# Another order of the steps of a fused RWKV attention and gated MLP kernel, with PSUM tiles of their own for idle bursts and for the last unit's halves

## The chip, the cores and the metric

The kernel runs on one core of a Trainium2 chip. The time is the device time of one execution in microseconds (us), and of several executions the median. Five engines work side by side, each in the order of its own queue: TensorE (PE: matmuls, with the weight loads shown apart as PEld), VectorE (DVE), ScalarE (ACT), GpSimd (POOL) and SyncE (SP, which here only issues DMAs). They wait for each other by semaphores.

## The reference

Two things are computed one after the other: a linear attention with a decaying state for 4 batches, 8 heads, 768 steps and a head width of 48, and a two-layer network on its result (3072 tokens, 384 wide, 2048 hidden).

```python
for t in range(S):
    cur = np.einsum('bhd,bhe->bhde', u[None] * kt, vt)
    y[:, :, t] = np.einsum('bhd,bhde->bhe', rt, state + cur)
    state = w[None, :, :, None] * state + np.einsum('bhd,bhe->bhde', kt, vt)
x = np.ascontiguousarray(attn_out.transpose(0, 2, 1, 3)).reshape(B * S, H * D)
h = x @ w_in
g = np.where(pos, h, np.where(neg, 0.0, (h + beta) ** 2 / (4.0 * beta)))
return (g @ w_out).astype(np.float32)
```

Here `pos` is h >= 1 and `neg` is h <= -1.

## The kernel before

**Tiles.** The 768 steps are cut into 6 chunks of 128. A *unit* is one chunk of one batch (24 of them, n = 0 to 23), a *group* is two units, one chunk of two batches (12 of them, g = 0 to 11; unit n belongs to group n // 2). Group g = 0 and 1 are the first chunk of all four batches. In a chunk the recurrence is matmuls: r and k are scaled by powers of w (Rs, Ks), transposed, multiplied into a 128x128 matrix A per head, masked (AT) and multiplied with v; the state is carried from chunk to chunk.

**Steps.** The whole program is a list of words, `ORDER` (lines 24 to 60). A loop at line 573 goes through it and calls for each word a function `do_...`, which issues the instructions of that step. So the place of a word in `ORDER` sets its place in the queue of its engine, and nothing reorders it later. `Ks1.0=G` is step Ks for group 1, unit half 0, on GpSimd; V, A and G stand for VectorE, ScalarE and GpSimd; the numbers behind a slash are the PSUM tiles that the step takes. A step waits for the data it reads and for the last reader of the tile that it takes. Some 680 words make the 4051 instructions.

The steps of a group, with the lines that the profile names:

- LR, LK, LV (line 253, SP's queue): loads of r, k, v, in two halves for the first groups, whole later.
- KU, RKU (282), us (304), V (308, the cast of v to bf16, line 112), B (313): the term with u. Rs, Ks (282): the scaled r and k.
- TR, TK, T (330, PE) with cR, cK, c (112): transposes of Rs and Ks for groups 0 to 2; later groups use DMA transposes RT, KT (318).
- A or AA (370, PE), AT (379, or 384 in halves; VectorE), Y (432, 438, PE), y or yg (446, 450; VectorE): the attention's result of a unit or group.
- Sp (405, PE), Tm or Tmg (409, 413; VectorE), decayg (416), sbf or sbfg: the state.
- X and xc (460, 112) or xcg (467, a DMA transpose): y transposed, as tile xT.
- m (475, PE): a quarter q of the hidden layer, 12 matmuls into tile hp; r (486 on ScalarE, 483 on VectorE as a clamp), s (495 or 493, ScalarE), g (498, VectorE): the activation; g reads hp last and frees it.
- M (512, PE): g times w_out for unit j and quarter q, into tile op; og, o (112): op to SBUF; stg, st (558, 555): the store.

`m4.0` is quarter 0 of group 4, `M4.01` is unit 0, quarter 1 of group 4.

**The head.** bw and bu (207, 211) spread log w and u over the partitions by matmuls, wq (233) makes the powers for the state; Wup, Wdn (215, 219) write exp tables to PSUM, WupS, WdnS (222, 225) to SBUF for later groups. WI and WO (244, 247) are the loads of the weights, in three parts each, cast on the way, from GpSimd's queue. `Z` (566) is a burst of matmuls on zeros into tile z.

**PSUM.** Two pairs of banks, p0 and p1, stand for the whole run. The other four banks are single ones, b0 to b3, until the first step takes pair 2 or 3; from then on they are those two pairs. All the steps above that use PSUM share the tiles by these numbers. In the last group the output of a unit has a tile of its own, and the last unit is computed in two halves of 192 columns (MA, MB, and M with both), which both lie in one tile; oA, oB copy them out, stA, stB store them.

Of the kernel before, what the change touches and what calls it, by code (L numbers as in the profile page):

```python
# [40 lines left out]
Sp9 AT11 Tmg4 m4.1/3 s4.0=A Y10/0 Y11 yg5 m4.2/2 r4.1 g4.0 xcg5 RT6 s4.1=A g4.1 m4.3/0 r4.2 us6 KT6 r4.3 LV8 s4.2=A  # L41
g4.2 M4.00/1 M4.10 M4.01 stg0 M4.11 s4.3=A g4.3 m5.1/3 Ks7=G V7 M4.12 LR8 decayg4=G Rs7=G AA6/02 M4.02 M4.03 M4.13
r5.1 AT12 m5.0/0 s5.1=A V6 sbfg4=A stg2 AT13 Y12/2 Y13 stg1 og4=V m5.2/1 g5.1 KU8=G B6=G yg6 m5.3/3 KT7 xcg6 Sp10/2
r5.0 s5.0=A KU7=G RKU7=G r5.2 s5.2=A Sp11 g5.0 M5.00/0 M5.10 M5.11 M5.01 RT7 Tmg5 LR9 g5.2 M5.02 Ks8=G LK9 us7 r5.3
s5.3=A V8 g5.3 decayg5=G sbfg5=A LK11 m6.1/2 r6.1 s6.1=A stg3 Rs8=G RT8 B7=G AA7/13 M5.03 Rs9=G M5.12 M5.13 AT15
m6.0/3 og5=A r6.0 AT14 g6.1 Y14/0 Y15 yg7 RKU8=G KU9=G xcg7 s6.0=A m6.3/1 m6.2/2 g6.0 Sp12/0 Sp13 r6.3 r6.2 s6.2=A us8
KT8 M6.00/3 M6.10 M6.11 M6.01 Tmg6 LV11 B8=G s6.3=A m7.1/0 RT9 LK10 g6.2 M6.02 LV10 g6.3 AA8/21 M6.03 r7.1 M6.12 M6.13
decayg6=G AT16 sbfg6=A RKU9=G LR10 s7.1=A AT17 Ks9=G og6=A m7.0/2 Sp14/1 Sp15 Y16/3 Y17 r7.0 g7.1 m7.2/0 KU11=G s7.0=A
Tmg7 yg8 xcg8 Ks10=G KT9 r7.2 m7.3/1 g7.0 M7.00/3 s7.2=A g7.2 M7.10 M7.11 LV9 r7.3 M7.01 KU10=G s7.3=A g7.3 V10 stg6
decayg7=G M7.12 RKU10=G sbfg7=A M7.02 AA9/02 M7.13 m8.0/1 stg5 LR11 AT18 Rs10=G V9 KT10 M7.03 r8.0 s8.0=A AT19 RT10  # L50
og7=V us9 B9=G m8.1/0 m8.2/2 r8.1 s8.1=A Y18/3 Y19 stg7 g8.0 m8.3/1 yg9 r8.2 Rs11=G RKU11=G M8.00/3 M8.10 xcg9 g8.1
M8.11 s8.2=A g8.2 Sp16/0 Sp17 Tmg8 stg4 RT11 r8.3 s8.3=A M8.01 M8.02 g8.3 m9.0/2 r9.0 s9.0=A us10 decayg8=G AA10/01
AT21 Ks11=G M8.03 sbfg8=A B10=G AT20 M8.12 M8.13 g9.0 og8=A m9.1/1 Y20/0 Y21 r9.1 m9.2/3 s9.1=A yg10 xcg10 g9.1 r9.2
M9.00/0 m9.3/2 KT11 s9.2=A stg8 M9.10 M9.11 Sp18/1 Sp19 r9.3 g9.2 s9.3=A M9.01 Tmg9 M9.02 g9.3 m10.0/3 decayg9=G V11
# [20 lines left out]
def kernel(  # L75
# [485 lines left out]
    def do_Zs(e, b):  # L561
        tiles["z"] = pair(b[0], F32, "z")

    def do_Z(e, b, n):
        for i in range(n):
            nc.tensor.matmul(tiles["z"][:, 0, :P], idle[:, :P], idle[:, :P], start=True, stop=True)  # L566

    def do_Zq(e, b, n):
        for i in range(n):
            nc.tensor.matmul(tiles["z"][:, 0, :D], idle[:, :P], idle[:, :D], start=True, stop=True)  # L570
# [40 lines left out]
```

## Time and profile before

| | us |
|---|---|
| median of 3 runs | 174.13 |
| lowest and highest | 174.08, 174.55 |
| span of the profiled execution | 172.6 |
| busy: PE, DVE, ACT, POOL | 164.4, 130.6, 129.9, 117.4 |

The page gives the span of the profiled execution, from its first to its last instruction, and no other time for it; the runs' median lies 1.5 us above the span. Busy times are sums over the span. A row of a timeline reads: start, length (us), engine, line, operation, out<-in, shapes, count, and in brackets the idle time ahead of it with what ended it. A row of a chain reads: start, length, what. The granted clock of TensorE is 1.00 throughout.

### The profile page before, as it was taken

The page shows a single profiled execution, that of the slowest core. Times are in us where ns is not written, and L with a number is a line of the kernel's source. Part 1 is how long each engine was busy: PE and PEld are TensorE (multiplying, and loading weights), DVE is VectorE, ACT ScalarE, POOL GpSimd, SP SyncE. Part 2 cuts the span into 40 slices and gives each one's busy share as a digit, 9 for nine tenths or more (in the row PEclk, how much of TensorE's full clock was granted, in tenths as well). Part 3 has the DMA queues.
Part 4 walks back from the last instruction along what each step waited for, and adds up shares of the span by engine and source line. Part 5 has one row for each costly group of instructions (what it writes and reads, how often), then busy time and mean ns, then how long its engine had stood idle before and what let it go on. Part 6 is the DMA issues. An engine that isn't in the chain of part 4 may idle for free.

```text
span 172.6 us, 4051 instructions
## 1 busy us (share of the span) xinstructions
PE 164.4 (95%) x1674; PEld 132.9 (77%) x1674; DVE 130.6 (76%) x150; ACT 129.9 (75%) x150; POOL 117.4 (68%) x86
## 2 busy tenths in 40 slices
...
GB/s 114 194 184 179 199 187 180 228 210 174 206 191 99 206 184 168 194 199 145 196 312 210 182 220 163 223 182 155 297 170 267 4 52 145 37 104 0 8 91 91
DMA packets 103751, 28.26 MB, mean 164 GB/s; under 512 B 98866, under 2 KB 102836, under 8 KB 103732
## 3 DMA queue, kind: packets, MB, share of 16 engines
...
q10 hardware_dynamic: 148, 0.10, 0.2%
...
## 4 chain that ended last, share of the span: by engine, by line
PE 87%; ACT 4%; DMA 2%; DVE 2%; issue 1%; POOL 0%; ACTq 0%; DVEq 0%
PE hp L475 35%; PE op L512 34%; PE A L370 4%; PE Y L438 3%; DMA xT<-y 2%; PE Y L432 2%; PE Sp L405 2%; PE z L566 2%; ACT pt L486 1%; PE T L330 1%; ACT TT L112 1%; PE lwp L207 1%; PE wp L233 1%; PE TR L330 1%; PE TK L330 1%
## 5 line engine op out<-in xcount | busy, mean ns | idle before, releaser
L475 PE MATMUL hp<-xT,w_in 128*128 128x256 bf16 x576 | 69.1, 273 | 1.3 <-DMA xT<-y 0.8
L512 PE MATMUL op<-w_out,g 128*128 128x384 bf16 (+1 forms) x400 | 68.4, 320 | 0.0
L498 DVE SCALAR_TENSOR_TENSOR g<-sq,hp 128x1024 bf16<-128x1024 bf16 x48 | 57.9, 1215 | 13.2 <-ACT sq L495 13.2
L475 PEld LDWEIGHTS <-w_in 128*128 128x128 bf16 x576 | 61.9, 114 | 4.6 <-issue 1.6
L486 ACT ACTIVATE pt<-hp 128x1024 f32<-128x1024 f32 x46 | 46.9, 1021 | 13.7 <-PE hp L475 13.7
L512 PEld LDWEIGHTS <-g 128*128 128x128 bf16 x400 | 37.5, 98 | 20.4
L495 ACT ACTIVATE sq<-pt 128x1024 bf16<-128x1024 f32 x46 | 48.3, 1057 | 1.2
L379 DVE TENSOR_TENSOR AT<-A,umask 128x1024 bf16<-128x1024 f32 x20 | 23.7, 1220 | 5.2 <-PE A L370 5.2
L282 POOL TENSOR_TENSOR Ks<-Ki,Wdn 128x768 bf16<-128x768 f32 (+1 forms) x12 | 20.3, 1689 | 8.5 <-ACT Wdn L225 3.4
L313 POOL TENSOR_TENSOR V<-Vb,diag 128x768 f32<-128x768 bf16 (+1 forms) x14 | 18.1, 1291 | 9.8 <-DVE diag L304 4.4
L282 POOL TENSOR_TENSOR RKU<-Ri,KU 128x768 f32<-128x768 f32 (+1 forms) x13 | 21.2, 1630 | 1.1 <-DVE KU L282 0.7
L282 POOL TENSOR_TENSOR KU<-Ki,u_sb 128x768 f32<-128x768 f32 (+1 forms) x13 | 21.2, 1634 | 0.4 <-DMA Ki<-in_k_dram 0.4
L416 POOL TENSOR_TENSOR state<-Tm,wCm 128x768 f32<-128x768 f32 x8 | 14.6, 1824 | 9.8 <-DVE Tm L413 9.8
L282 POOL TENSOR_TENSOR Rs<-Ri,Wup 128x768 bf16<-128x768 f32 x10 | 18.2, 1820 | 0.3 <-DMA Ri<-in_r_dram 0.3
L112 ACT CAST Vb<-Vi 128x768 bf16<-128x768 f32 (+1 forms) x14 | 10.2, 733 | 5.4 <-DMA Vi<-in_v_dram 5.4
L450 DVE TENSOR_TENSOR y<-Y,V 128x768 bf16<-128x768 f32 x10 | 9.6, 956 | 5.9 <-PE Y L438 3.3
L304 DVE TENSOR_REDUCE diag<-RKU 128x16 f32<-128x768 f32 (+1 forms) x14 | 11.6, 831 | 1.5 <-POOL RKU L282 1.5
L112 ACT CAST state_bf<-state 128x768 bf16<-128x768 f32 (+1 forms) x12 | 8.5, 717 | 4.4 <-POOL state L416 4.4
L112 ACT COPY o<-op 128x768 f32<-128x768 f32 (+1 forms) x9 | 6.7, 748 | 6.0 <-PE op L512 5.9
L438 PE MATMUL Y<-Vb,AT 128*128 128x48 bf16 x192 | 10.4, 186 | 0.4 <-ACT Vb L112 0.4
L438 PEld LDWEIGHTS <-AT 128*128 128x128 bf16 x192 | 9.5, 98 | 0.7 <-issue 0.5
L413 DVE TENSOR_TENSOR Tm<-Sp,state 128x768 f32<-128x768 f32 x8 | 7.7, 956 | 3.1 <-PE Sp L405 3.1
...
## 6 DMA issues: line engine op xcount, KB each, us to landing
...
Ki<-in_k_dram SPq DMA_DIRECT2D x6, 192.0 KB, 4.0
Ri<-in_r_dram SPq DMA_DIRECT2D x6, 192.0 KB, 4.7
Vi<-in_v_dram SPq DMA_DIRECT2D x6, 192.0 KB, 6.0
...
```

Of the source, the lines that this page charges most:

```text
L112: nc.scalar.copy(out, in_) if e == "A" else engines[e].tensor_copy(out, in_)
L282: engines[e].tensor_mul(part(out)[:, :, :, :D], part(a), rep(b, j1 - j0) if len(b.shape) == 3 and b.shape[1] == H else part(b))
L304: nc.vector.tensor_reduce(d[:, hs], tiles["RKU", g][:, hs, :], AX.X, ALU.add)
L313: engines[e].tensor_mul(t[:, hs, :], tiles["V", g][:, hs, :], tiles["diag", g][:, hs].unsqueeze(2).to_broadcast([P, n, D]))
L379: nc.vector.tensor_mul(t.rearrange("p i n t -> p (i n) t"), tiles["A", n].rearrange("p i (n t) -> p (i n) t", t=P), umask.unsqueeze(1).to_ ...
L416: engines[e].tensor_mul(states[g % BP], tiles["Tm", g], flat(wCm).unsqueeze(1).to_broadcast([P, UNITS, DM]))
L438: nc.tensor.matmul(Y[:, h * D : (h + 1) * D], AT[:, i, p, :], V[:, j * H + h, :], start=(c == 0), stop=True, skip_group_check=True,)
L475: nc.tensor.matmul(hp[:, f, :], w_in_sb[wi][:, i, wo * FG * P + f : (wo + 1) * FG * P : FG], tiles["xT", g][:, :, i, :], start=(i == 0), s ...
L486: nc.scalar.activation(t, tiles["hp", g, q], AF.Relu, bias=0.5, scale=0.5)
L495: nc.scalar.activation(t, p, AF.Square)
L498: nc.vector.scalar_tensor_tensor(out=make("g", ("g", g, q), [P, FG, TOK], BF16), in0=tiles["sq", g, q], scalar=1.0, in1=tiles["hp", g, q], ...
L512: nc.tensor.matmul(tiles[key][:, i, : o1 - o0], tiles["g", g, q][:, f, j * P : (j + 1) * P], w_out_sb[wi][:, wo, f * DO + o0 : f * DO + o1 ...
```

## The change

All words of `ORDER` are put in another order, and some steps change their engine. The numbers of steps per engine, before and after: VectorE 138 and 154, ScalarE 149 and 141, GpSimd 76 and 67, PE 235 and 233, SP 83 and 84. VectorE gets, of steps that others did, three Ks, one Rs, two RKU, two decayg, three B, the clamps r1.3, r4.2, r9.0, r10.3 and r11.1 (r1.2 goes), most of the early copies cR and cK, and oA; it gives og4 and og10 to ScalarE. GpSimd casts V0.0 and V1.1 (so far all casts of v were on ScalarE).

The list up to the first output matmuls, around group 4's transposed y, and at the end:

```diff
-Zs/0 ln Z19 bw/1 LK0.0 bu/0 uS=V LK1.0 LR0.0 LK0.1 LR0.1 LV0.0 wq/2 WdnS Ks1.0=G LR1.0 LR1.1 Wdn/3 Ks0.0=V Ks0.1=V
-TK0/0 Wup/1 Rs0.0=V TR0/3 LK1.1 cK0=A WupS KU0.1=G KU0.0=V RKU0.0=G cR0=A KU1.0=G LV0.1 Rs0.1=V Z2 TR1/1 A0/03 LV1.0
-LV1.1 WI0 WI1 WI2 us0.0 cR1=A TK1/1 cK1=A AT0.1 Z4 A1/13 Rs1.0=V LR2.0 LR2.1 Rs1.1=V V0.1 AT1.0 V0.0 Z9 TR3/1 B0.0=G
-AT1.1 RKU0.1=V wE AT0.0 wC=A us0.1 Z7 Y1/3 TR2/0 B0.1=G Y0/2 y0 y1 cR2=A RKU1.0=G Z8 X0/2 Z4 TK2/3 X1/0 Ks1.1=G xc0=A
-Sp1/2 cK2=A xc1=A Z7 TK3/3 cK3=A Tm1 A2/20 m0.0/0 cR3=V us1.0 AT2.1 AT2.0 r0.0=A A3/31 AT3.1 KU1.1=G RKU1.1=G m0.1/1
-V1.0 s0.0=A B1.0=G Sp2/2 AT3.0 us1.1 r0.1=A Tm2 Y2/3 y2 g0.0 V1.1 X2/0 LK2.0 Y3/1 B1.1=G s0.1=A LK2.1 Sp0/2 Sp3/3
-xc2=V LK3 y3 WO0 WO1 m0.3/0 r0.3=A s0.3=A g0.1 X3/1 Tm0 xc3=V m0.2/1 LR3 LV2.0 Tm3 m1.1/2 g0.3 r1.1=V m1.0/3 m1.2/0
-Ks2=G r0.2=A s0.2=A g0.2 sbf2=A s1.1=A r1.0=A s1.0=A sbf3=A g1.1 m1.3/1 r1.2=V WO2 KU2=G LV2.1 M0.00/2 M0.10 M0.11
+ln=A LR0.1 LK0.0 Z17/0 bu/1 LR0.0 LK0.1 LV0.1 LV0.0 bw/3 uS=V KU0.0=V LK1.0 LK1.1 Wup=A/1 RKU0.0=V Wdn=A/0 KU0.1=G
+RKU0.1=G us0.0=V V0.0=G wq/2 Ks0.1=V Ks0.0=V Rs0.0=V LR1.0 wE=A WdnS=A Rs0.1=V WupS=A Zp16/0 TR1/1 V0.1=A us0.1=V
+TK1/0 TR0/3 B0.1=V cR1=V B0.0=V Ks1.0=V wC=A cR0=A TK0/1 WI0 Ks1.1=V LR1.1 LV1.0 KU1.1=G cK0=A cK1=V KU1.0=G LV1.1
+Z5/2 A0/21 A1/30 AT0.0=V LK2.0 AT1.0=V AT1.1=V Rs1.0=V WI1 AT0.1=V LK2.1 Zp9/0 Y1/2 Sp0/3 TK3/0 LR2.1 LR2.0 Y0/1 Tm0=V
+cK3=V y1=V LR3 y0=V Zp10/1 X1/2 X0/0 TR2/1 RKU1.0=G V1.0=A xc1=A us1.0=V cR2=V Rs1.1=G WI2 V1.1=G WO1 TK2/2 xc0=A
+Zp3/0 TR3/1 cK2=V RKU1.1=V LK3 Sp2/3 LV2.0 A2/20 LV2.1 LV3 cR3=A m0.0/0 r0.0=A AT2.0=V Tm2=V AT2.1=V s0.0=A A3/13
+AT3.1=V B1.0=V Y2/2 m0.1/1 AT3.0=V y2=V Z9/0 X2/3 g0.0=V Sp1/1 r0.1=A s0.1=A Y3/0 xc2=V us1.1=V m0.3/0 B1.1=G g0.1=V
+y3=V r0.3=A Sp3/3 X3/2 Tm1=V xc3=V m0.2/1 LK4 LK5 LV5 LR4 Tm3=V s0.3=A WO0 m1.1/3 r0.2=A WO2 LR5 m1.0/2 g0.3=V s0.2=A
+r1.1=V s1.1=A sbf1=A r1.0=A g0.2=V s1.0=A Ks2=G KU2=G g1.1=V m1.2/0 m1.3/1 M0.11/3 RKU2=G r1.3=V g1.0=V Rs2=V r1.2=A
+s1.3=A s1.2=A M0.01 M0.00 M0.10 M1.11/2 M1.01 M0.03 M0.12 M0.02 g1.2=V g1.3=V T5/0 M0.13 T4/1 sbf2=A c5=A M1.10 A5/0
+c4=A M1.12 us2=V A4/1 Rs3=G Ks3=V KU3=G AT5=V sbf0=A og0=A M1.13 M1.02 T6/0 AT4=V c6=V V2=A B2=G Y5/3 Sp5/1 Y4 Sp4
 ...
-LV6 r3.0 s3.0=A Ks5=G g2.3 M2.03 Sp6/3 Sp7 M2.13 g3.0 m3.2/0 Rs5=G Tmg3 r3.1 s3.1=A RT5 og2=A g3.1 V4 AA4/23 AT9 Ks6=G
-r3.2 s3.2=A KT5 m3.3/1 M3.00/3 M3.10 V5 B4=G AT8 Y8/2 Y9 r3.3 g3.2 s3.3=A LK8 M3.11 M3.12 M3.01 M3.02 yg4 AA5/20 g3.3
-M3.13 M3.03 xcg4 m4.0/1 LR7 KU5=G RKU5=G AT10 LK7 decayg3=G sbfg3=A Rs6=G og3=A us5 LV7 B5=G KU6=G RKU6=G r4.0 Sp8/2
+m3.3/3 AT9=V M3.01/0 M3.00 LV4 KT5 LK6 RT5 LK8 AT8=V decayg3=G V4=A r3.2=A s3.2=A g3.2=V Y8/2 r3.3=A Y9 V5=A B4=G
+yg4=V M3.10 M3.12 s3.3=A M3.11 M3.02 AA5/21 xcg4 sbfg3=A RKU5=G g3.3=V M3.13 M3.03 us5=V KU6=G AT11=V AT10=V m4.0/3
 ...
-m11.1/0 M10.02 M10.03 r11.1 s11.0=A m11.2/1 g11.0 M10.12 M10.13 s11.1=A r11.2 g11.1 m11.3/2 og10=V s11.2=A M11.10/0
-M11.11 g11.2 stg10 r11.3 s11.3=A M11.00/3 M11.01 M11.12 M11.02 g11.3 M11.03 MA11.13 MB11.13 o11.0=V st11.0 oA11.1=A
-stA11.1=A oB11.1=V stB11.1
+m11.2/0 s10.3=A r11.0=A s11.0=A g10.3=V M10.03 g11.0=V m11.1/2 r11.1=V r11.2=A M10.10 M10.12 m11.3/3 M10.13 M10.02
+s11.2=A g11.2=V M11.02/0 M11.00 s11.1=A g11.1=V r11.3=A s11.3=A M11.01 g11.3=V og10=A M11.10/12 M11.11 MA11.13 M11.03
+M11.12 o11.0=V stg10 st11.0 MB11.13 oA11.1=V oB11.1=V stA11.1 stB11.1
```

In the code, the cast of v takes its engine from the list; the last unit's halves get a PSUM tile each, and the first matmul of an accumulation is found by counting, since the quarters may come in any order; an idle burst takes a tile when it runs (Z a single bank in the head, Zp a pair) where before one tile of pair 0 was taken once by Zs:

```diff
-        copy("A", t[:, hs, :], tiles["V32", g][:, hs, :])
+        copy(e or "A", t[:, hs, :], tiles["V32", g][:, hs, :])
...
-        key = ("op", g, j) if last else ("op", g)
-        if key not in tiles:
-            tiles[key] = pair(b[0], F32, "op")
...
         for i, o0, o1 in [(i, i * DO // 2, (i + 1) * DO // 2) for i in halves] if last and j else [(j, 0, DO)]:
+            key = ("op", g, j, i) if last else ("op", g)
+            if key not in tiles:
+                tiles[key] = pair(b.pop(0), F32, "op")
+            n = counts["op", g, j, i] = counts.get(("op", g, j, i), 0) + 1
...
-                    start=(q == 0 and f == 0), stop=(q == nQ - 1 and f == FG - 1),
+                    start=(n == 1 and f == 0), stop=(n == nQ and f == FG - 1),
...
-    def do_Zs(e, b):
-        tiles["z"] = pair(b[0], F32, "z")
+    def idling(t, n):
+        for i in range(n):
+            nc.tensor.matmul(t, idle[:, :P], idle[:, :P], start=True, stop=True)
...
     def do_Z(e, b, n):
-        for i in range(n):
-            nc.tensor.matmul(tiles["z"][:, 0, :P], idle[:, :P], idle[:, :P], start=True, stop=True)
...
+        idling(pair(b[0], F32, "z")[:, 0, :P] if later else bank(b[0], [P, P], F32, "z"), n)
+
+    def do_Zp(e, b, n):
+        idling(pair(b[0], F32, "z")[:, 0, :P], n)
```

The bursts before are Z19, 2, 4, 9, 7, 8, 4 and 7 (60 matmuls), after Z17, Zp16, Z5, Zp9, Zp10, Zp3 and Z9 (69).

More of the change, by code (lines that the diff above doesn't have):

```diff
@@ L40 @@
-M3.13 M3.03 xcg4 m4.0/1 LR7 KU5=G RKU5=G AT10 LK7 decayg3=G sbfg3=A Rs6=G og3=A us5 LV7 B5=G KU6=G RKU6=G r4.0 Sp8/2
[L41 to L54, printed above, removed]
@@ new lines @@
+decayg5=G r5.2=A M5.11/1 s5.2=A g5.2=V RT7 xcg6 r5.3=A us7=V M5.01 M5.00 M5.10 s5.3=A V7=A m6.1/2 M5.02 Rs8=G KU8=G
+sbfg5=A r6.1=A g5.3=V B7=G Ks8=G s6.1=A AA7/03 AT15=V AT14=V M5.13 M5.03 M5.12 m6.0/3 LK9 LR10 Y14/0 Y15 g6.1=V LK10
+RT8 LV8 LR9 yg7=V og5=A m6.2/1 Sp12/2 r6.0=A m6.3/0 s6.0=A g6.0=V Sp13 r6.2=A KU9=G Rs10=G RKU8=G xcg7 KT8 M6.10/3
+M6.01 M6.11 M6.00 s6.2=A r6.3=A g6.2=V Tmg6=V s6.3=A g6.3=V M6.02 m7.1/1 AA8/02 us8=V V8=A r7.1=A M6.12 M6.13
+decayg6=G B8=G Ks9=G RKU9=G AT16=V AT17=V s7.1=A M6.03 sbfg6=A Rs9=G m7.0/0 og6=A Y17/3 KU10=G Sp15/2 g7.1=V Y16
@@ new lines @@
+sbfg8=A s9.0=A og8=A m9.1/0 Y21/3 Y20 r9.1=A g9.0=V m9.2/1 yg10=V s9.1=A g9.1=V RKU11=G r9.2=A M9.10/2 m9.3/3 us11=V
+Sp19/0 s9.2=A M9.01 M9.11 Sp18 r9.3=A stg8 M9.00 KT11 stg5 xcg10 RT11 g9.2=V Tmg9=V s9.3=A g9.3=V M9.02 m10.0/0 B11=G
+AA11/13 decayg9=V AT23=V r10.0=A sbfg9=A s10.0=A M9.03 M9.13 M9.12 AT22=V m10.1/3 og9=A g10.0=V Y22/1 Y23 m10.2/0
+r10.1=A yg11=V s10.1=A xcg11 stg7 m10.3/2 stg9 g10.1=V r10.2=A M10.00/1 M10.11 M10.01 r10.3=V s10.2=A g10.2=V m11.0/3
+m11.2/0 s10.3=A r11.0=A s11.0=A g10.3=V M10.03 g11.0=V m11.1/2 r11.1=V r11.2=A M10.10 M10.12 m11.3/3 M10.13 M10.02
@@ L528, in half_out @@
     def half_out(e, g, j, i):
-        copy(e, make("o", ("o", g, j, i), [P, UNITS, DO], F32)[:, 0, : DO // 2], tiles["op", g, j][:, i, : DO // 2])
+        copy(e, make("o", ("o", g, j, i), [P, UNITS, DO], F32)[:, 0, : DO // 2], tiles["op", g, j, i][:, i, : DO // 2])
     def do_oA(e, b, g, j):
```

26 lines of the change are left out of this document (14 added, 12 removed).

## The prediction

> **What bounds the kernel now.** The page first: the span, and who is busy in it.
>
> ```profile
> span 172.6 us, 4051 instructions
> PE 164.4 (95%) x1674; PEld 132.9 (77%) x1674; DVE 130.6 (76%) x150; ACT 129.9 (75%) x150; POOL 117.4 (68%) x86
> ```
>
> The 95% of PE is an average over two very different stages, so the chain that ended last comes next, in order of time (start, length, what), and then the table by stage.
>
> ```profile
> 27.27 6.73 PE hp L475 x60
> ...
> 68.81 0.96 DVE y L450
> 69.80 4.27 DMA xT<-y
> 74.11 1.47 PE hp L475 x12
> ...
> 169.14 0.33 ACT o L112
> 169.49 0.36 DVE o L112
> ```
>
> ```profile
> 10.73:27.27 16.54, 14.29 (x180) 12.68 (x179) 13.84 (x25) 10.26 (x19) 10.81 (x14) 1.00 1.12 187
> 27.27:69.10 41.83, 41.83 (x438) 33.57 (x438) 34.04 (x35) 35.12 (x41) 34.84 (x21) 1.00 1.09 185
> 74.10:163.86 89.76, 89.75 (x922) 73.48 (x922) 69.95 (x66) 75.62 (x80) 61.48 (x36) 1.00 0.82 156
> ```
>
> The columns after the length of the stretch are PE, PEld, DVE, ACT, POOL busy. From 27.27, where step m0.2 starts, PE is busy 41.83 of 41.83 and 89.75 of 89.76 us. In that part no order of steps can gain more than PE's idle time there, and the view of PE's waits after 27 us has, beside m0.2's own wait for g0.1, one row:
>
> ```profile
> PE hp L475 <- DMA xT<-y: 0.8, 1, 0.8
> ```
>
> That is m4.0 at 74.11, which waits for group 4's transposed y. So three things can move the end: when the gap-free part is entered, the 0.84 us before 74.11, and the 3.5 us after PE's last matmul. Before 27.27 PE is not the bound: the idle bursts keep it busy with nothing. VectorE is: 13.84 of 16.54 us.
>
> **Part 1, the entry: a sum along VectorE.** In the new order m0.2 stands behind X3, which needs y3, which stands in VectorE's queue behind g0.1. I add up VectorE's queue up to y3. In-order work without waits costs the step from one start to the next, which is less than the duration that a row shows:
>
> ```profile
> 8.27 0.55 DVE L282 TENSOR_TENSOR KU<-Ki,u_sb 128x384 f32<-128x384 f32 x1
> 8.74 0.54 DVE L282 TENSOR_TENSOR Rs<-Ri,up_t 128x384 bf16<-128x384 f32 x1
> ...
> 18.74 0.41 DVE L112 COPY TT<-TR 128x512 bf16<-128x512 bf16 x1
> 19.07 0.54 DVE L304 TENSOR_REDUCE diag<-RKU 128x8 f32<-128x384 f32 x1
> 19.53 1.28 DVE L384 TENSOR_TENSOR AT<-A,umask 128x512 bf16<-128x512 f32 x2
> ...
> 26.00 1.21 DVE L498 SCALAR_TENSOR_TENSOR g<-sq,hp 128x1024 bf16<-128x1024 bf16 x1
> ```
>
> Steps: a half product 0.47 (8.27 to 8.74), a cR or cK 0.33 (18.74 to 19.07), a us 0.46, an AT half 0.60 (two in 1.28, the last lasting 0.68), an xc taken like a cR; a g its full 1.21.
>
> The sum starts at Ks0.1, which needs the fourth load (its issue, and the time to landing of the loads in flight at 2.65) and dn_t (pieces of the chain, and ACT's timeline):
>
> ```profile
> 2.65 0.82 SPq L253 DMA_DIRECT2D Ki<-in_k_dram  x1
> Ki<-in_k_dram SPq DMA_DIRECT2D x1, 192.0 KB, 4.4
> ```
>
> ```profile
> 3.44 1.64 PE lwp L207 x2
> 5.09 1.28 PE up L211 x2
> ...
> 5.60 0.55 ACT L219 ACTIVATE dn_t<-lwp,dn_col 128x384 f32<-128x384 f32 x1
> ```
>
> LK0.1 is fourth in SP's queue in both orders, so it lands at 2.65 + 4.4 = 7.05. The new order puts bu ahead of bw; with u_row there by about 3.0, bw ends near 3.0 + 1.64 + 1.28 = 5.9 instead of 5.08, and the second exponential, dn_t, ends 1.06 after that (as 5.60 + 0.55 = 6.15 comes 1.06 after 5.09), at 6.95. The 0.8 us lost by that swap is hidden by the load. Ks0.1 starts at 7.1.
>
> From Ks0.1 to y3 VectorE gets 17 half products and sums (four Ks, three Rs, one RKU, three B, four y, two Tm): 17 x 0.47 = 8.0; three us 1.4; eight AT halves 4.8; five cR/cK 1.65; two g 2.4; one xc 0.35. Together 18.6, so y3 would end at 25.7 without a wait. Waits that I find by setting the queues beside each other: 0.25 at AT0.0 (A0 now stands behind four sets of transposes and Z5, four matmuls of 0.107 us each, see the idle bursts below), 0.4 at cR2 (TR2 behind Zp10, X1 and X0), 0.2 at cK2 (TK2 waits for the bank that ACT reads in xc1), 0.15 in small ones: 1.0. So y3 ends at 26.7, X3 starts at 26.75, m0.2 at 26.9 (three transposes, 0.17). Against 27.27 that is **0.37 us earlier**. Bounds: no wait at all, 1.0 earlier still; each of these 36 operations at its full duration (0.08 more apiece), 2.9 later. I take the steps, since they are measured in a queue as full as this one.
>
> What else the entry needs. WI2 has to be there for m0.3, which must end by 26.75:
>
> ```profile
> 10.79 2.48 POOL L244 DMA_DIRECT2D w_in<-in_moe_w_in_dram  x3
> w_in<-in_moe_w_in_dram POOLq DMA_DIRECT2D x1, 768.0 KB, 12.6
> q0 software_dynamic: 1200, 1.57, 62.5%
> ```
>
> Before, the three issues stand together and the last lands at 12.4 + 12.6 = 25.0, 14.2 us after the first issue, for the 1.57 MB of q0 in that window: 0.11 MB/us. After, POOL has KU0.1, RKU0.1 and the V0.0 cast ahead of WI0, two KU ahead of WI1, RKU1.0 and Rs1.1 ahead of WI2: issues near 9.9, 13.3 and 16.1. A transfer of 0.39 MB takes 3.5 us at that rate, so each issue comes about when the transfer before it ends, and the last lands between 9.9 + 14.2 = 24.1 and 25 again. Cost 0, but if it came at 26 the entry would come a us later. POOL's cast of a half V is not in the trace: VectorE's half copy (0.41 at 18.74) and POOL's half product (0.99 at 9.85, below) bound it; I take 0.82, POOL's half B, and the time between WI0's landing and m0.0 hides it. V1.1 is twelfth in SP's queue in both orders; POOL's cast of it and B1.1 end by 25.9, before y3 is reached. V0.1 rises from tenth to fifth load, LR1.1 falls from eighth to tenth, and POOL asks for it only at 15.1.
>
> **Part 2, the middle.** VectorE gets four more clamps (as wide as a g, 1.21), six full products that POOL did and two fewer output copies (both taken as a y, 0.96): 4.8 + 5.8 - 1.9 = 8.7 us more in 131.6, on 104.0 busy (34.04 + 69.95): 86%. POOL and ACT get less. So no engine passes PE. The new queues are tightest around 36 us, where g1.0 ends some 0.15 before M1.11 wants its pair. The wait before 74.11: between Y9 and m4.0 stand six M, an AA: 4.45 us, the same list in both orders, against 0.96 + 0.03 + 4.27. It stays. In the other groups at least 4.57 us stand there, against 0.99 and a median of 3.0:
>
> ```profile
> xT<-y SPq DMA_TRANSPOSE x9, 3.0
> ```
>
> I take 0 for the middle; bounds: 0.84 less, 1.5 more.
>
> **Part 3, the end.** oA reads a tile that MB writes after it was ready, so ACT starts it at 169.14, after MB, and oB follows it at 169.49. With a tile for each half, oA needs only the first half's matmuls and ends before MB does; oB starts at 169.14. **0.35 us less.** og10, which M11.10 waits for, stands behind r11.3 and s11.3 on ACT and ends some 2.95 us after m11.3; five M of 0.65 stand before M11.10, 3.25. The margin is 0.3.
>
> The sum: -0.37 + 0 - 0.35 = -0.7 on 172.6, so a span of 171.9. The page gives no time for the profiled execution but its span; the median, 174.13, lies 1.5 above it, and with that 1.5 kept the time is **173.4**. Less than 0.3% (0.5 us) can't be told from no change.
>
> **The rivals.** *VectorE and POOL in each other's way.* Before, VectorE's products with both inputs in SBUF fall where POOL does no arithmetic, but for one pair of rows (below a half product of POOL, and the group of a full one):
>
> ```profile
> 9.85 0.99 POOL L282 TENSOR_TENSOR KU<-Ki,u_sb 128x384 f32<-128x384 f32 x1
> ...
> 13.93 0.55 DVE L282 TENSOR_TENSOR RKU<-Ri,KU 128x384 f32<-128x384 f32 x1
> 14.36 0.82 POOL L313 TENSOR_TENSOR V<-Vb,diag 128x384 f32<-128x384 bf16 x1 [1.10 <-ACT w_col L236]
> ```
>
> ```profile
> L282 POOL TENSOR_TENSOR Rs<-Ri,Wup 128x768 bf16<-128x768 f32 x10 | 18.2, 1820 | 0.3 <-DMA Ri<-in_r_dram 0.3
> ```
>
> The last two of the timeline overlap by 0.12 us, with usual durations, which says little; POOL's full product takes 1.82. The new order puts such products beside POOL's work: B0.1 beside the V0.0 cast, Ks1.1 beside KU1.1 (both released by one load), Rs1.0 beside RKU1.0. If whichever starts second has to wait, VectorE loses 0.3, 0.9 (part of a 0.99 us KU) and 0.85 less what its waits above swallow, some 1.6 us, straight into y3, and Rs2 and Ks3 can lose up to 1.82 each behind full POOL products near 36 to 41 us, where there is no margin. That gives 173.4 + 1.6 = 175.0. It decides from 0.4 us of blocking on. The Trainium skill, SBUF — State Buffer, section "Who interferes with whom", states it as a rule: a VectorE instruction with two SBUF inputs and a GpSimd instruction that reads SBUF exclude each other, and the second waits for the whole of the first. By that rule the time is 175.0; no run here shows it yet. I give it 0.3.
>
> *PE still at half clock when m0.0 comes.* The idle bursts show the change:
>
> ```profile
> 15.87 1.03 PE L566 MATMUL z<-idle 128*128 128x128 bf16 x8
> ...
> 18.00 0.55 PE L566 MATMUL z<-idle 128*128 128x128 bf16 x7
> ```
>
> Less the last one's own 0.28 and 0.22, eight stand 0.107 apart and the later seven 0.055. If that came 2 us later, m0.0 would take 1.3 longer: 174.7. Against it: as dense a PE from 12 us on as before. 0.06.
>
> *Nothing to be seen*: VectorE waits 0.4 more in the head, or the middle gives back what the end gains: 174.0. Half a dozen hand-overs between engines in the head that I set right behind each other speak for it. 0.22.
>
> *More*: the wait before 74.11 goes as well, with loads in another order beside group 4's transfer: 172.6. 0.12.
>
> **Numbers.** The forecast 0.30 (its own range 172.9 to 173.6), more 0.12, nothing 0.22, blocking 0.30, half clock 0.06. Faster 0.42, same 0.22, slower 0.36. The range takes in "more" and blocking with a little of the middle's: 172.4 to 175.6.
>
> **What would show it.** y3 ending at 26.7 and m0.2 starting at 26.9; the half product still 0.47 apart on VectorE beside a busy POOL (a Ks1.1 or Rs1.0 that lasts over 0.6 or starts late without another cause is the blocking); WI2 landing by 25; one PE wait of 0.8 before m4.0; oA over before MB ends. I am wrong if m0.2 starts after 27.3, or if PE shows waits of over 0.3 between 27 us and the last unit other than m4.0's.

## The result and the profile after

The kernel after takes **179.02 us** (median of 4 runs, 178.53 to 180.34) against 174.11 us for the kernel before (4 runs): a ratio of 1.0288, 95% interval 1.0247 to 1.033. It is slower; the prediction said 173.4 and a range up to 175.6. Medians here are of all executions; the ratios leave out single executions in a slower state, of which a0 (182.43) and f2 (184.16) below had one each. The head of the profiled execution (178.53 us) reads:

```profile
span 176.5 us, 4053 instructions
PE 164.7 (93%) x1683; PEld 132.3 (75%) x1683; DVE 145.7 (83%) x166; ACT 125.3 (71%) x143; POOL 105.3 (60%) x77
...
PE 68%; DVE 17%; ACT 5%; DMA 4%; issue 3%; ACTq 0%; DVEq 0%
```

From m0.2 on PE does the same work, in a span 3.9 us longer; the third line is the chain that ended last by engines, in which VectorE had 2% before and now has 17%. The table by stage from m0.2's start to PE's last matmul, first of the kernel before, then of the kernel after (length, then PE, PEld, DVE, ACT, POOL busy):

```profile
27.27:169.10 141.83, 140.99 (x1442) 113.40 (x1441) 111.14 (x106) 113.94 (x123) 101.24 (x59) 1.00 0.88 163
```

```profile
29.00:173.25 144.25, 141.49 (x1443) 112.83 (x1440) 120.48 (x113) 112.03 (x122) 91.74 (x53) 1.00 0.83 155
```

The 3.9 us of the span split by these rows: m0.2 starts at 29.00 in place of 27.27 (**+1.73**); PE is idle 2.76 us behind it in place of 0.84 (**+1.92**) and busy 0.50 longer; from PE's last matmul to the span's end it takes 3.25 in place of 3.5 (-0.25). Why PE is busy 0.50 longer was not followed up. The median moved by a further 1.0: 0.5 is that the profiled execution was the fastest of the four (178.53 against 179.02), and 0.5 that its time lies 2.0 above its span, where the median before lay 1.5 above the span of an execution whose own time is not on record.

**The entry.** The timeline of the kernel after, VectorE's rows first, then POOL's and PE's (in brackets the idle time ahead of a row and what ended it):

```profile
8.46 1.01 DVE L285 TENSOR_TENSOR Rs<-Ri,up_t 128x384 bf16<-128x384 f32 x2
...
11.31 2.62 DVE L285 TENSOR_TENSOR Ks<-Ki,Wdn 128x384 bf16<-128x384 f32 x2
13.85 0.41 DVE L115 COPY TT<-TK 128x512 bf16<-128x512 bf16 x1
...
16.16 0.55 DVE L285 TENSOR_TENSOR Rs<-Ri,Wup 128x384 bf16<-128x384 f32 x1
...
28.06 0.55 DVE L449 TENSOR_TENSOR y<-Y,V 128x384 bf16<-128x384 f32 x1
```

```profile
11.20 2.31 POOL L285 TENSOR_TENSOR KU<-Ki,u_sb 128x384 f32<-128x384 f32 x2 [0.74 <-DMA Ki<-in_k_dram]
...
16.19 0.80 POOL L247 DMA_DIRECT2D w_in<-in_moe_w_in_dram  x1
```

```profile
14.32 0.61 PE L373 MATMUL A<-TT 48*128 48x128 bf16 x8 [1.73 <-DVE TT L115]
```

Two half products on VectorE take 1.01 us when one input lies in PSUM (the look-up table `up_t`), and 2.62 when both lie in SBUF (Ks1.0 and Ks1.1, table `Wdn`) and POOL multiplies beside them. The copy cK1 stands behind the pair, and PE stands 1.73 us for it before A1. Rs1.0, with the same kind of inputs, takes its usual 0.55 at 16.16: POOL is issuing a DMA just then.

**The middle.** PE's waits behind 28 us, where the kernel before had one of 0.8 (the third row ends the entry: X3 for y3):

```profile
PE op L515 <- DVE g L501: 1.2, 1, 1.2
PE hp L478 <- DMA xT<-y: 0.9, 1, 0.9
PE X L463 <- DVE y L449: 0.7, 1, 0.7
PE Y L435 <- DVE o L115: 0.5, 1, 0.5
```

The timeline around the first of them:

```profile
59.50 1.84 POOL L285 TENSOR_TENSOR KU<-Ki,u_sb 128x768 f32<-128x768 f32 x1
59.57 2.58 DVE L285 TENSOR_TENSOR RKU<-Ri,KU 128x768 f32<-128x768 f32 x1
61.30 2.52 POOL L285 TENSOR_TENSOR Rs<-Ri,Wup 128x768 bf16<-128x768 f32 x1
62.08 1.21 DVE L501 SCALAR_TENSOR_TENSOR g<-sq,hp 128x1024 bf16<-128x1024 bf16 x1
...
63.34 0.99 PE L515 MATMUL op<-w_out,g 128*128 128x384 bf16 x5 [1.20 <-DVE g L501]
```

RKU4, a full product with two SBUF inputs, takes 2.58 us on VectorE; the gate behind it is late, and so is PE. When POOL is at rest such a product takes 0.95: Rs2 and Ks3, for which the prediction had feared. POOL has nothing to do from 36.6 to 38.5 and from 40.5 to 46.0, and where its KU3 overlaps the end of Rs2 by 0.34, it is KU3 that takes 2.02 in place of 1.83:

```profile
37.88 0.95 DVE L285 TENSOR_TENSOR Rs<-Ri,Wup 128x768 bf16<-128x768 f32 x1
42.37 0.95 DVE L285 TENSOR_TENSOR Ks<-Ki,Wdn 128x768 bf16<-128x768 f32 x1
```

```profile
34.75 1.83 POOL L285 TENSOR_TENSOR Rs<-Ri,Wup 128x768 bf16<-128x768 f32 x1
38.49 2.02 POOL L285 TENSOR_TENSOR KU<-Ki,u_sb 128x768 f32<-128x768 f32 x1 [1.91 <-DMA Ki<-in_k_dram]
45.96 1.48 POOL L316 TENSOR_TENSOR V<-Vb,diag 128x768 f32<-128x768 bf16 x1 [5.45 <-ACT Vb L115]
```

The wait of 0.9 is for the transposed y of group 7, not of group 4 as before. Two pieces of the chain that ended last:

```profile
106.54 4.95 DMA xT<-y
111.54 1.50 PE hp L478 x12
```

**The clock.** The table by stretches of 1 us (last columns: granted clock, DMA share, GB/s):

```profile
14.00:15.00 1.00, 0.68 (x10) 0.49 (x11) 0.90 (x3) 0.00 (x0) 0.98 (x2) 0.66 1.23 231
15.00:16.00 1.00, 1.00 (x10) 0.84 (x8) 1.00 (x2) 0.00 (x0) 1.00 (x2) 0.50 1.29 228
```

PE stands still from 12.6 to 14.3, and right behind it the granted clock falls to 0.50 until about 17.7. The kernel before is at half clock there too (its idle bursts stand 0.107 us apart up to 17), and VectorE, on which the entry hangs, has between 10 and 28.6 us only two waits of over 0.15 us for PE, of 0.27 and 0.17. So this stretch explains little of the later entry; what did lengthen the entry is the pair.

### The profile page after: what moved, and what is told of

It is laid out like the page before. It is cut to its first block, busy times and chain, and to the rows that moved or that the text cites. A ratio compares the mean times of both kernels' runs of the same rounds, so it can differ in the third digit from the quotient of the medians.

```text
span 176.5 us, 4053 instructions
## 1 busy us (share of the span) xinstructions
PE 164.7 (93%) x1683; PEld 132.3 (75%) x1683; DVE 145.7 (83%) x166; ACT 125.3 (71%) x143; POOL 105.3 (60%) x77
## 3 DMA queue, kind: packets, MB, share of 16 engines
HBM read 20.45 MB, written 4.72 MB: 143 GB/s over the span
## 4 chain that ended last, share of the span: by engine, by line
PE 68%; DVE 17%; ACT 5%; DMA 4%; issue 3%; ACTq 0%; DVEq 0%
PE op L515 29%; PE hp L478 27%; DVE g L501 4%; PE A L373 3%; DMA xT<-y 3%; ACT pt L489 2%; DVE Ks L285 2%; PE Y L441 2%; PE Y L435 2%; DVE AT L387 2%; DVE RKU L285 1%; PE Sp L408 1%; ACT sq L498 1%; DVE AT L382 1%; DMA u_row<-in_u_dram 1%
## 5 line engine op out<-in xcount | busy, mean ns | idle before, releaser
L489 ACT ACTIVATE pt<-hp 128x1024 f32<-128x1024 f32 x42 | 42.9, 1021 | 14.3 <-PE hp L478 14.1
L498 ACT ACTIVATE sq<-pt 128x1024 bf16<-128x1024 f32 x42 | 44.4, 1057 | 1.2
L316 POOL TENSOR_TENSOR V<-Vb,diag 128x768 f32<-128x768 bf16 (+1 forms) x11 | 15.6, 1418 | 21.7 <-DVE diag L307 12.4
L285 POOL TENSOR_TENSOR KU<-Ki,u_sb 128x768 f32<-128x768 f32 (+1 forms) x13 | 21.8, 1680 | 7.3 <-DVE RKU L285 4.7
L285 POOL TENSOR_TENSOR RKU<-Ri,KU 128x768 f32<-128x768 f32 (+1 forms) x11 | 19.2, 1743 | 1.0 <-DMA Ri<-in_r_dram 0.8
L419 POOL TENSOR_TENSOR state<-Tm,wCm 128x768 f32<-128x768 f32 x6 | 11.0, 1827 | 11.7 <-DVE Tm L416 11.6
L285 POOL TENSOR_TENSOR Ks<-Ki,Wdn 128x768 bf16<-128x768 f32 x9 | 16.4, 1829 | 0.0
L285 POOL TENSOR_TENSOR Rs<-Ri,Wup 128x768 bf16<-128x768 f32 (+1 forms) x9 | 16.3, 1812 | 0.0
L115 ACT COPY o<-op 128x768 f32<-128x768 f32 x10 | 8.0, 802 | 6.1 <-PE op L515 6.1
L115 ACT CAST Vb<-Vi 128x768 bf16<-128x768 f32 (+1 forms) x12 | 9.1, 774 | 4.0 <-DMA Vi<-in_v_dram 4.0
```

Of the source, the lines that this page charges most:

```text
L115: nc.scalar.copy(out, in_) if e == "A" else engines[e].tensor_copy(out, in_)
L285: engines[e].tensor_mul(part(out)[:, :, :, :D], part(a), rep(b, j1 - j0) if len(b.shape) == 3 and b.shape[1] == H else part(b))
L316: engines[e].tensor_mul(t[:, hs, :], tiles["V", g][:, hs, :], tiles["diag", g][:, hs].unsqueeze(2).to_broadcast([P, n, D]))
L419: engines[e].tensor_mul(states[g % BP], tiles["Tm", g], flat(wCm).unsqueeze(1).to_broadcast([P, UNITS, DM]))
L489: nc.scalar.activation(t, tiles["hp", g, q], AF.Relu, bias=0.5, scale=0.5)
L498: nc.scalar.activation(t, p, AF.Square)
```

## The experiments

My theory from here on was: VectorE and POOL hold each other up where a VectorE instruction has two SBUF inputs, at the places named; the rivals: the wait for loads and transposes, the order as such, the clock, the tail. Ratios are to the kernel before on the same chip.

**e1: the pair's tables from PSUM.** Both tables of the first units get a PSUM tile that stays; Ks1.0, Ks1.1 and Rs1.0 read them there. Nothing else changes.

```diff
-        t = tiles["up_t"] = pair(b[0], F32, "up_t")[:, 0, :DM]
+        both = pair(b[0], F32, "up_t")
+        t, tiles["dn_t"] = both[:, 0, :DM], both[:, 1, :DM]
...
-        t = tiles["dn_t"] if g == 0 and "dn_t" in tiles else flat(Wdn)
+        t = tiles["dn_t"] if (g == 0 or g == 1 and e == "V") and "dn_t" in tiles else flat(Wdn)
```

> The new order with one thing changed: VectorE's products of group 1 in the head (Ks1.0, Ks1.1, Rs1.0) read the exp tables from PSUM, where group 0's products read them already, and no longer from SBUF; order, engines and sizes stay. Theory (a VectorE product with both inputs in SBUF and a GpSimd product exclude each other): the pair Ks1.0, Ks1.1 falls from 2.62 us to about 1.0, A1 and all of VectorE's queue behind it come 1.6 us earlier, m0.2 starts near 27.4 instead of 29.0, TensorE's wait of 1.7 for cK1 goes; the time falls from 179.0 by 1.6 or more, to 177.4 or below. Rival (VectorE's queue is simply too long, or the swap of bw and bu and TensorE's half clock near 15 us cost it): the pair stays at 2.6 us or the gain is taken back, 178.6 to 179.4.

Measured: 176.85 us, ratio 1.0137 (1.0082 to 1.0192). The timeline of VectorE, and of PE at the entry:

```profile
11.32 1.01 DVE L287 TENSOR_TENSOR Ks<-Ki,up_t 128x384 bf16<-128x384 f32 x2
```

```profile
27.36 6.73 PE L480 MATMUL hp<-xT,w_in 128*128 128x256 bf16 x60
```

(The row names `up_t` because both tables now lie in that tile.) The pair is back at 1.01 with POOL's two KU beside it as before, the 1.73 us wait is gone, the half clock behind it too, and m0.2 comes 1.64 us earlier: the 1.61 that the pair lost. About half of the loss (2.9% to 1.4%) hangs on this one pair. What is left is mostly the middle: m0.2 is now only 0.09 later than in the kernel before.

**e2 and e3: the full products back on POOL**, without and with e1's edit. Rs2, Ks3, RKU4, Rs7, decayg7 and decayg9, of which RKU4 is typical (the "one Rs" and "two RKU" told of the change are net: Rs1.1 and RKU0.1 went from VectorE to POOL):

```diff
-m3.1/3 RKU4=V r2.3=A
+m3.1/3 RKU4=G r2.3=A
```

> The new order with the six full products Rs2, Ks3, RKU4, Rs7, decay of groups 7 and 9 back on GpSimd, at their places in the list. Theory (RKU4 took 2.58 us and decay7 1.92 on VectorE, where 0.95 is usual, because GpSimd held the way to SBUF): TensorE's waits of 1.2 us for a g near 63 us and 0.5 us near 130 us go, the time falls by 1.2 to 1.7, to 177.3 to 177.8. Rival (those waits come from the order of the steps itself and from the late entry): the waits stay or move, and GpSimd, with 11 us more to do, brings new ones: 178.7 to 180.5.

> The edits of the two runs before in one kernel. Theory: the gains add, 3 us, to about 176.0; what is left over 174.1 is the wait of 0.9 for group 8's transposed y, the other waits of the order and what the head still loses. Rival: under 1 us of gain, 178 or more.

Measured: e2 179.89, ratio 1.0318 (1.0254 to 1.0382); e3 178.01, ratio 1.018 (1.0117 to 1.0244). Undoing the engine change in the middle gains nothing that the times show, with the entry mended or not: e2 took as long as the kernel after in a0 below (179.87), e3 more than e1, but for one execution (176.18). RKU4 no longer holds VectorE up, but POOL, which comes to this part late, has more to do, and PE waits for a gate that stands behind POOL's result. The matmuls behind the longest wait of e3, and the table by stretches of 1 us from there:

```profile
65.19 2.69 PE L480 MATMUL hp<-xT,w_in 128*128 128x256 bf16 x12 [1.97 <-DVE g L503]
```

```profile
65.00:66.00 1.00, 0.81 (x5) 0.58 (x5) 1.00 (x3) 0.83 (x1) 0.00 (x0) 0.63 1.28 269
66.00:67.00 1.00, 1.00 (x6) 0.71 (x5) 1.00 (x2) 0.00 (x0) 0.85 (x1) 0.50 1.43 192
```

Behind the wait PE is at half clock for about 3.4 us, here where PE is the bound: twelve matmuls take 2.69 us. Three of e3's runs show a mean clock of 0.99 and took 177.93 to 178.22 us; the fourth shows 1.00 and took 176.18. One such stretch, half of whose 3.4 us is lost, fits that difference of some 1.9. The wait alone doesn't bring it: the profile of e2 has a wait of 2.0 us at the same place, and f1's below one of 1.98, and the granted clock behind both is 1.00.

**e4: the end alone.** The kernel before with the change's code for the last unit's halves (`M11.10/03`, and the tile key `("op", g, j, i)`), in its own order.

> The kernel before with only the last unit's halves in PSUM tiles of their own (M11.10 takes pairs 0 and 3, M11.00 pair 1), nothing else moved. Theory: the copy of the first half starts before the last matmuls end, the copy of the second right behind them instead of 0.35 us later, and the time falls by 0.35, to 173.75. Rival: the stores' landing or the new wait of M11.10 for og10 takes it back: 174.0 to 174.3.

Measured: 174.27, ratio 0.9993 (0.9967 to 1.002), the rival's side. ACT's copy starts ahead of MB's end, as the prediction said:

```profile
168.92 0.32 ACT L112 COPY o<-op 128x192 f32<-128x192 f32 x1 [2.86 <-PE op L512]
```

It was 169.14. The last store went out 0.23 earlier (169.64 against 169.87), which can't be told from nothing in the time.

**a0: the kernel after once more**, on the chip of the next runs.

> The new order as it is, beside the runs below on one chip. Both theories: 178.5 to 179.5, with the pair Ks1.0, Ks1.1 at 2.6 us, RKU4 at 2.58 and TensorE at half clock for one or two windows of 3.4 us after its wait for cK1.

Measured: 179.87 (179.30 to 182.43), ratio 1.0312 (1.0296 to 1.0328). The loss stands on another chip. The profiled execution is the one of 182.43, and in it the same products are held up by other amounts: the pair took 1.82 in place of 2.62, Rs1.0 1.96 in place of 0.55, and RKU4 4.38, through two full products of POOL that kept their 1.85 and 1.84:

```profile
60.31 4.38 DVE L285 TENSOR_TENSOR RKU<-Ri,KU 128x768 f32<-128x768 f32 x1
```

**f1: e1 with only RKU4 and decayg7 back on POOL**, the two products of the middle that were held up.

> The tables in PSUM as in the first run, and of the six full products only the two that were seen to be held up, RKU4 (2.58 us) and decay7 (1.92), back on GpSimd. Theory (what is lost in the middle is the holding-up of these two on VectorE): the wait of 1.2 us near 61 us goes and the time falls from 176.85 to about 175.5. Rival (GpSimd has no room for them there: returning all six brought a wait of 2.0 us near 65 us instead of the 1.2): RKU4 on GpSimd makes its queue late, TensorE waits 1.5 to 2 us for a g near 65 us and may fall to half clock for a window, 177 to 178.5.

Measured: 176.67, ratio 1.014 (1.0124 to 1.0155), the same as e1 and not the 175.5 that I expected. The wait of 1.2 behind RKU4 is replaced by 2.0 behind POOL. PE's row behind that wait (at full clock: 1.47 for twelve matmuls) and POOL's timeline, which shows from where it comes:

```profile
65.43 1.47 PE L480 MATMUL hp<-xT,w_in 128*128 128x256 bf16 x12 [1.98 <-DVE g L503]
```

```profile
44.33 1.48 POOL L318 TENSOR_TENSOR V<-Vb,diag 128x768 f32<-128x768 bf16 x1 [4.72 <-ACT Vb L115]
...
61.45 1.81 POOL L287 TENSOR_TENSOR RKU<-Ri,KU 128x768 f32<-128x768 f32 x1
```

POOL is idle 4.72 us for V2's cast on ACT, and from 44.33 eleven products stand end to end, the last of them RKU4 at 61.45, for which VectorE and then PE wait. From this trace alone it looks as if the new order needed VectorE's help there because POOL starts late; f4 and f5 below show another way out.

**f2: an idle burst in the entry's wait.** `Zp24/0` between A0 and A1, to keep the clock up.

> The new order with 24 more idle matmuls between A0 and A1, where TensorE stands for 1.7 us and then falls to half clock for 3.4 us. Nothing else changes, so VectorE is held up as before. Theory (VectorE's queue is what sets the entry, the half clock lies beside it): the granted clock stays at 1.00 from 11 us on, but the gain is 0.5 us at most: 178.4 to 179.2. Rival (the half clock is itself what costs): 1.5 us less, 177.0 to 177.7.

Measured: 180.54, ratio 1.0357 (1.0341 to 1.0373). Neither number came. The timeline of VectorE:

```profile
11.13 1.82 DVE L285 TENSOR_TENSOR Ks<-Ki,Wdn 128x384 bf16<-128x384 f32 x2
...
15.48 1.49 DVE L285 TENSOR_TENSOR Rs<-Ri,Wup 128x384 bf16<-128x384 f32 x1
```

The pair, untouched by the edit, took 1.82 this time, and Rs1.0, now beside a POOL product, 1.49 in place of 0.55; half clock came all the same, from 18.5 to 22. So f2 doesn't decide what the half clock costs. How much the pair loses depends on what happens to lie side by side.

**g1: the load that stands ahead of the transpose.** In the kernel before, LK8 goes behind xcg4 in SP's queue, against the 0.84 us before m4.0.

```diff
-s3.3=A LK8 M3.11
+s3.3=A M3.11
...
-xcg4 m4.0/1
+xcg4 LK8 m4.0/1
```

> The kernel before with one load, LK8, moved from just ahead of group 4's transposing DMA (xcg4) to just behind it in SyncE's queue. In the profile before, that transpose takes 4.27 us against a median of 3.0 and TensorE waits 0.84 us for it. Theory (the load's 384 KB in front of it in the same queue make it late): the wait falls to nothing or 0.3, the time by 0.5 to 0.8, to 173.4. Rival (the DMA engines are full anyway, with what was queued earlier): the wait stays at 0.7 to 1.0 and the time within 0.2.

Measured: 174.51, ratio 1.0021 (1.0003 to 1.004). That wait goes, and one of 0.63 for the transposed y of the next group comes, at 82.69. No gain, and neither the theory's time nor the rival's wait.

**p1: the pair by itself.**

> The disputed step by itself: six products of 128x384 f32 into bf16 in each of five stretches; the whole computation is left out and zeros are written into 128 rows of the output. In order: VectorE alone with both inputs in SBUF, VectorE alone with one input in PSUM, POOL alone, VectorE with one input in PSUM beside POOL, VectorE with both inputs in SBUF beside POOL. My theory (the two engines take turns only where the VectorE product has two SBUF inputs): 0.47 a step, 0.47, 0.95, both at those steps side by side, and in the last stretch a VectorE product waits for a whole POOL product or the other way round, some 1.4 us for a pair, 2.8 us or more over what the fourth stretch takes. The rival (the 2.62 us of the pair in the kernel after came from something else, a load or a wait that the trace puts down to the product): the last stretch takes as long as the fourth, six POOL steps.

The timeline: VectorE with both inputs in SBUF before POOL starts, then both engines with VectorE's second input in PSUM (six products each), then both with all inputs in SBUF (two products of each, of six):

```profile
2.81 1.42 DVE L109 TENSOR_TENSOR dv<-a,c 128x384 bf16<-128x384 f32 x3
...
13.45 5.76 POOL L111 TENSOR_TENSOR po<-a,c 128x384 bf16<-128x384 f32 x6 [2.34 <-ACT c L115]
13.71 2.88 DVE L109 TENSOR_TENSOR dv<-a,q 128x384 bf16<-128x384 f32 x6 [3.83 <-ACT q L116]
...
21.26 1.31 POOL L111 TENSOR_TENSOR po<-a,c 128x384 bf16<-128x384 f32 x1
21.64 1.34 DVE L109 TENSOR_TENSOR dv<-a,c 128x384 bf16<-128x384 f32 x1
22.53 1.30 POOL L111 TENSOR_TENSOR po<-a,c 128x384 bf16<-128x384 f32 x1
22.90 1.34 DVE L109 TENSOR_TENSOR dv<-a,c 128x384 bf16<-128x384 f32 x1
```

With both inputs in SBUF and POOL at rest, VectorE needs 0.47 a product (1.42 for three). With one input in PSUM it needs 0.48 beside POOL, which needs 0.96: they don't feel each other. With both in SBUF they go in step, one product of each every 1.27 us (21.26 to 22.53, 21.64 to 22.90): VectorE at 1.34 in place of 0.47, POOL at 1.31. This is the price that the kernel after shows, where VectorE's two took 2.62. It comes here without any load or other step of the kernel, which were the rival's causes. One product of each costs a little less than I expected (0.47 + 0.96 = 1.43), and six of each 7.33 us on POOL against 5.76, 1.6 more and not 2.8.

The Trainium skill, SBUF — State Buffer, section "Who interferes with whom", says that a VectorE instruction with two SBUF inputs and a GpSimd instruction that reads SBUF exclude each other, and that the second waits for the whole of the first. The trace agrees on the condition, and nearly on the price: 1.27 for one of each is 0.16 less than one product of each end to end, so they overlap by that much.

**f3, f4, f5, f6: the waits one by one.** Each takes the kernel ahead of it, from f1 on, and moves the steps that its trace shows PE's waits to hang on.

```diff
 f3
-sbf0=A og0=A M1.13 M1.02 T6/0 AT4=V c6=V V2=A B2=G Y5/3
+sbf0=A V2=A og0=A M1.13 M1.02 T6/0 AT4=V c6=V RKU3=G B2=G Y5/3
...
-xc4=A RKU3=G og1=A
+xc4=A og1=A
...
-RT8 LV8 LR9 yg7=V
+RT8 LV8 yg7=V
...
-xcg7 KT8
+xcg7 LR9 KT8
 f4
-us1.0=V cR2=V
+us1.0=V RKU1.1=V cR2=V
...
-cK2=V RKU1.1=V LK3
+cK2=V us1.1=V LK3
...
-us1.1=V m0.3/0 B1.1=G g0.1=V
-y3=V
+m0.3/0 B1.1=G y3=V g0.1=V
 f5
-cR2=V Rs1.1=G WI2
+cR2=V WI2 Rs1.1=G
...
-us4=V r3.1=A
+r3.1=A
...
-g3.1=V og2=A
+g3.1=V us4=V og2=A
...
-xcg7 LR9 KT8
+xcg7 KT8 LR9
 f6
-RKU3=G B2=G Y5/3
+B2=G RKU3=G Y5/3
```

> The kernel f1 (look-up tables of the first units read in PSUM, the fourth RKU product and decay 7 on POOL) with three moves: V2's cast ahead of og0 on ScalarE, RKU3 ahead of B2 on POOL, LR9 behind xcg7 in SP's queue. My theory: each is what the wait left in f1 hung on, so the waits of 2.0 us (for a gate, behind the POOL chain that starts late at V2) and of 1.0 us (for xcg7's transposing load) go and nothing takes their place: 176.67 less about 2.6, 174.0, equal to the kernel before. Rival: the loss moves on, to another wait of the same order whose covers are as thin: over 175.5.

> f3 with three VectorE steps of the entry moved: RKU1.1 right behind us1.0, us1.1 behind cK2, y3 ahead of g0.1. If the entry hangs on VectorE's order there, the last fc1 strip of the first unit starts at 26.7 to 27.0 us instead of about 27.4, and the time is 0.4 to 0.7 below f3's, about 173.4, faster than the kernel before. Rival: the stores that go out earlier put the loads of K2 and R2 off, or the next wait takes it back: no gain over f3.

Measured: f3 176.43, ratio 1.012 (1.0093 to 1.0148), the rival's side. f4 175.62, ratio 1.0079 (1.0054 to 1.0104): 0.8 below f3, and m0.2 starts at 26.49, in place of f3's 27.24, so the entry does hang on VectorE's order (m0.2 is what the expectations call the last fc1 strip of the first unit); but f3, from which f4 starts, lay 2.4 above my 174.0, and f4 is not faster than the kernel before. The wait that stayed in both, in f4's timeline:

```profile
60.87 1.81 POOL L287 TENSOR_TENSOR RKU<-Ri,KU 128x768 f32<-128x768 f32 x1
...
62.72 0.95 DVE L309 TENSOR_REDUCE diag<-RKU 128x16 f32<-128x768 f32 x1 [3.10 <-POOL RKU L287]
...
63.59 1.21 DVE L503 SCALAR_TENSOR_TENSOR g<-sq,hp 128x1024 bf16<-128x1024 bf16 x1
...
64.85 1.47 PE L480 MATMUL hp<-xT,w_in 128*128 128x256 bf16 x12 [1.81 <-DVE g L503]
```

The reduce us4 stands ahead of the gate in VectorE's queue and waits 3.10 us for POOL; PE waits for the gate. What costs the time there is less POOL's lateness than what stands behind it: f5 moves us4 behind a gate, and this wait is gone.

> The kernel f4 with three steps moved, each for a wait that f4's trace still shows: us4 behind g3.1 on VectorE (TensorE waits 1.8 us near 63 us for a gate that stands behind us4, which waits for POOL's RKU4 to end at 62.7), WI2 ahead of Rs1.1 on POOL (0.6 us at 24.2 for w_in), LR9 behind KT8 in SP's queue (0.7 us at 110.3 for KT8). My theory: the new order loses by such waits alone, so 175.62 less 1.8, 0.6 and 0.7 is 172.5, and with something given back at most 173.4: faster than the kernel before. Rival: what the order lacks is VectorE and POOL time as such, so the waits come back elsewhere: over 174.5.

> The kernel f5 with B2 ahead of RKU3 on POOL again, as in the kernel after (f3 had put RKU3 first because V2's cast came late; in f5 the cast ends at 43.0 and POOL comes to this place at 43.7). In f5 the last fc1 strip of the first unit starts 0.9 us earlier than in the kernel before, and TensorE gives it back in a wait of 1.1 us at 46.9 for y5, which stands behind B2. My theory: the waits are places in the order and nothing else, so this one goes, RKU3's reduce still finds it done at 48.7, and the time is 174.50 less 0.8 to 1.1, 173.4 to 173.7, faster than the kernel before by about 0.4%. Rival: the first 50 us are bound by the loads and by VectorE and POOL together, a wait of the same size comes up by 70 us, and the time stays at 174.3 or over.

Measured: f5 174.50, ratio 1.0015 (0.9996 to 1.0035), level with the kernel before, short of the 172.5 to 173.4 that I expected. The 1.8 and the 0.7 went, the 0.6 for w_in stayed, and a wait of 1.1 for y5 came at 47. POOL's timeline shows the first link:

```profile
33.26 1.81 POOL L287 TENSOR_TENSOR Ks<-Ki,Wdn 128x768 bf16<-128x768 f32 x1 [11.72 <-DMA Ki<-in_k_dram]
```

Ks2, which waits for its k, started at 31.04 in f4 and at 29.27 in the kernel after. POOL issues the last loads of w_out at 20.2 in f4 and f5 and at 27.9 in the kernel after; that these loads put the one of k off (f4's rival said so of stores) is read from these times and not tested. f6 puts B2, for which y5 waited, first again: **173.75**, ratio **0.9976** (0.996 to 0.9992), a little above the 173.4 to 173.7 that I expected. The entry and the waits of f6, with nothing above 0.3 behind the entry:

```profile
26.59 7.03 PE L480 MATMUL hp<-xT,w_in 128*128 128x256 bf16 x60
```

```profile
PE hp L480 <- DMA w_in<-in_moe_w_in_dram: 0.6, 1, 0.6
...
PE op L517 <- DVE AT L384: 0.3, 1, 0.3
```

So the new order, with the tables in PSUM, two products back on POOL and these moves, can hold a gain at the entry (m0.2 at 26.59 in place of 27.27), and f6 beats both kernels, the one before by 0.24%, which is small, with 1 outside of the interval. VectorE and POOL still meet in f6 (POOL's RKU2 takes 2.40 and KU3 2.54 in place of 1.81), but no wait of PE over 0.3 comes of it.

## Why the prediction was wrong, point by point

**What bounds the kernel**: right. PE is gap-free in the middle when nothing is late, and 3.65 of the span's 3.9 us are a later entry (1.73) and waits of PE (1.92).

**Part 1, the entry (-0.37 expected, +1.73 measured)**: the failed step is "17 x 0.47 = 8.0": the half product at 0.47 on VectorE also for Ks1.0 and Ks1.1. They took 2.62 in place of some 1.0 beside POOL's two KU, and e1, which changes only where their table lies, brings m0.2 from 29.00 to 27.36. The rest of the sum held as a total: Ks0.1 started at 7.52 in place of 7.1 (PE had u's row at 3.53, not at 3.0), and from there y3 ended 21.09 later, 19.5 without the pair's 1.61, against 19.6 in the sum. Even without the pair's loss, then, the start of Ks0.1 would have taken back the 0.37. I had measured 0.47 "in a queue as full as this one", but with POOL at rest or a table in PSUM. WI2 did no harm: in f4, where it stands at the same place in the list, PE's wait for it ends at 24.8, inside the range given, and in the kernel after it landed near 25.1 (16.19 + 8.9) and PE did not wait for it.

**The rival of VectorE and POOL (0.30, 175.0)**: the mechanism was right and told with its place, and should have been the forecast. That its price for the head, some 1.6, is also what the pair lost is luck: the items were 0.3 for B0.1, 0.9 for Ks1.1 and 0.85 for Rs1.0, and in the profile after B0.1 and Rs1.0 lost nothing, while Ks1.0, which seemed free, and Ks1.1 stood beside a KU each. The middle was not in its price at all: it feared for Rs2 and Ks3, which met a POOL at rest; RKU4 (2.58), decayg7 (1.92) and the gate behind RKU4 were the ones hit.

**Part 2, the middle (0 expected, bounds -0.84 and +1.5; +1.92 idle and 0.50 more PE time measured)**: "It stays", of the wait before m4.0, was wrong: it went, and one of 0.94 came at m7, where I had let "at least 4.57 us" stand against a median transfer of 3.0. PE had some 6.2 us of work there, but y ended at 105.43, the transfer was issued at 106.54, behind the load LR9, and took 4.95; f3, which puts LR9 behind the transfer, has 0.2 left of this wait. "So no engine passes PE" was right as an average and said nothing of single places: RKU4 at 2.58 us makes the gate behind it late, and PE waits 1.20 for it. The failed step here is the 0 for the middle. That RKU4 was slow because of POOL is read from the trace, by the price that p1 shows; no run gave RKU4 an input in PSUM. f3 to f6 mended the middle by moving single steps, with RKU4 and decayg7 on POOL.

**Part 3, the end (-0.35 expected)**: the mechanism was right, the size too large: 0.25 in the profile after, 0.23 in e4's trace, and nothing that can be told in e4's time.

**Half clock (0.06)**: it was asked only for m0.0, and there PE was at full clock (twelve matmuls in 1.50 at 21.06). In the entry it came between 14.3 and 17.7, where the kernel before has it too. In the middle, behind a wait of 1.97, it fits the 1.9 us between e3's runs.

Not settled: why the same pair took 2.62 us in one execution and 1.82 in others (f2, a0); why a wait of PE of about 2 us is followed by half clock in one execution and not in another; and the 1.0 by which the median moved more than the span. The two slower runs of the first four show a mean clock of 0.981 in place of 0.99; e2's profile, at 0.981 too, has half clock from about 15 to 22 us, about twice 3.4, which fits a second such stretch.
